# Moving the making of a bias column from the head of the program into the middle of a LayerNorm

## Chip, cores, metric

One core of one Trainium2 chip. The metric is the device time of one execution in microseconds, all four layers from inputs in HBM to the output in HBM. A profile's span runs from the program's first instruction to its last; the device time is about 1.8 us more.

In lines of the profile, PE is TensorE's matmuls and PEld its weight loads, DVE is VectorE, ACT ScalarE, POOL GpSimd and SP SyncE; L588 is line 588 of the kernel, often that of a helper. LN is LayerNorm, FFN the feed-forward block B.

## The reference

Two kinds of residual block alternate, A B A B, on x of 2048 x 448 in bf16.

```python
x = x + _A_ref(_layernorm(x), A_w_r, A_w_i)        # irfft2(rfft2(LN(x)) * W)
x = x + _B_ref(_layernorm(x), B_w1, B_b1, B_w2, B_b2)   # FFN with squared ReLU
x = x + _A_ref(_layernorm(x), A_w_r, A_w_i)
x = x + _B_ref(_layernorm(x), B_w1, B_b1, B_w2, B_b2)

def _B_ref(x, w1, b1, w2, b2):
    h = einsum("bsd,df->bsf", x, w1) + b1
    r = where(h > 0, h, 0)
    return einsum("bsf,fd->bsd", r * r, w2) + b2
```

"Layer 1" below is the first A and the first B, "layer 2" the second pair.

## The kernel before

The program is not written in the order in which it runs. Every operation is entered with what it reads and writes; a scheduler in the kernel then sorts the operations into one fixed list for each engine, from priorities (`PR`), from letters that say which engine may do an operation (`EN`), and from costs that it assumes. On the chip each engine works through its list in order and waits on semaphores. The scheduler also fills gaps of TensorE with matmuls on a tile of ones ("fillers", line 1157), to keep its clock up.

The parts that matter here are the transfers at the head, the small unit that turns b1 (14 rows of 128) into a column for each of the 14 blocks of F, and the loop of the first LN:

```python
        dma("act", FA_sb[:], dc["FA"])                           # 64 KB
        dma("act", b1r, B_b1.rearrange("(f p) -> f p", p=P))     # 3.5 KB
        dma("act", J_sb[:], dc["J"])                             # 32 KB, exchange matrix
        for e, a, b in (("sp", 0, 2), ("sp", 2, 4), ("sp", 4, 8), ("sp", 8, 12), ("sp", 12, 16)):
            dma(e, x_sb[:, a:b, :], x_dram[:, a:b, :], slow=1.5)
        # ...
        def b1_columns():
            q = _Tile(1)
            mm(q[lambda b: ps[:, b, 0:FB]], b1r, J_sb[0:FB, P - FB:P][:, ::-1], True, True)
            cp(b1T[:, 0:FB], q[lambda b: ps[:, b, 0:FB]])
        # ...
        for q in range(8):                     # LN of layer 1, two tiles at a time
            rank("A1", 0, q)
            ln_stats([2 * q, 2 * q + 1], True) # VectorE; tiles 1, 3, 11 on ScalarE
            ln_rstd([2 * q, 2 * q + 1])
            first_A(2 * q)                     # Fs = FA * rstd, 5 matmuls, evacuation to XA
            first_A(2 * q + 1)
        rank("aux", 0, 0)
        b1_columns()
        spectral(True)
```

`FA_sb`, `TD_sb` and `TI_sb` hold constant matrices of the transforms: Fs is FA scaled for one tile of x, XA takes what the matmuls with Fs give, a matmul with TD opens the spectral stage, and one with TI comes after it. `b1T` is first used by the FFN of layer 1. In the lists that the scheduler made, the b1 matmul stands behind TensorE's sixth filler, and the copy is the fourth instruction of VectorE, ahead of all statistics.

Of the kernel before, what the change touches and what calls it, by code (L numbers as in the profile page):

```python
# [10 lines left out]
P = 128  # L11
# [8 lines left out]
FB = 14  # L20
# [95 lines left out]
EN = {'lny': ['addbdbadb', 'aadbdadbb'], 'A1x': ['brxprrdr'], 'A1f': ['xrpxprbp'], 'A1e': ['abbbbaab'], 'A2s': ['dbbabbabadbbbddb'], 'A2e': ['abaabababdaadbaa'], 'TDe': ['adbbababb', 'abadaaaad'], 'Be': ['bbbabbbaa', 'abaaabaaa'], 'Bie': ['baaaadaab', 'aaaaabbda'], 'TIe': ['adbbbbaaa', 'aabdabbbb'], 'fle': ['badababdb', 'bddaabaab']}  # L116
# [77 lines left out]
def _res(a):  # L194
    return a.ap() if isinstance(a, _PsAP) else a
# [303 lines left out]
def _free(ap):  # L499
    n = 1  # L500
    for step, cnt in list(ap.ap)[1:]:
        n *= cnt
    return n


def bass_interleave_layers__spectral_gfnet__dense_activation_squared_relu__prompt_kernel(nc, A_x, A_w_r, A_w_i, B_x, B_w1, B_b1, B_w2, B_b2, out):
# [6 lines left out]
    with ExitStack() as es:  # L513
        onchip = set()

        def sb(name, shape, dt=BF16):
            t = es.enter_context(nc.sbuf_tensor(name, shape, dt))
            onchip.add(t.name)
            return t
# [10 lines left out]
        xb = arena[:, 2 * FB * 512:2 * FB * 512 + NT * D].rearrange("p (t d) -> p t d", t=NT)  # L530
# [15 lines left out]
        J_sb = sb("J_sb", [P, P])  # L546
        Fs = sb("Fs", [P, NFS, 2 * P])
        m2 = sb("m2", [P, NT, 4])
        ones = sb("ones", [P, P])
        W1_sb = sb("W1_sb", [P, 4, FF])  # L550
        b1r = Z[0:FB, 7, 3, 0:P]
# [10 lines left out]
        ps = es.enter_context(nc.psum_tensor("ps", [P, NB, 512], FP32))  # L562
# [24 lines left out]
        def mm(o, lhsT, rhs, start, stop, skip=False, half=False, unit=None):  # L587
            op = sch.add("pe", lambda e: e.matmul(_res(o), lhsT, rhs, start=start, stop=stop, skip_group_check=skip),  # L588
                         [lhsT, rhs], [o], cost=max(_free(rhs) / 2.4 + 2.5, 48.0) * (0.5 if half else 1.0), lat=195.0,
                         unit=unit)  # L590
            if half:
                op.mode = "half"
            return op
# [21 lines left out]
        def rank(k, L=None, n=None):  # L615
            if L is not None:
                at[:] = L, n
            sch.bias = PR[k][at[0]][at[1]]

        def evac(o, i, key):  # L620
            engs = ENG[EN[key][at[0]][at[1]]]
            rank(key)
            n = _free(o)
            far = isinstance(i, _PsAP)
            c = {"act": (n + (61.0 if far else 112.0)) / 1.2, "dve": n / 0.96 + 69.0 if far else n / 3.84 + 60.0,
                 "pool": n + 69.0}
            h = []
            op = sch.add("act", lambda e: e.activation(o, _res(i), ACT.Copy) if h[0].eng == "act" else  # L628
                         e.tensor_copy(o, _res(i)), [i], [o], cost=c["act"])  # L629
            h.append(op)  # L630
            op.alt = {e: c[e] for e in engs}

        def scaled(o, i, s, key):
            engs = ENG[EN[key][at[0]][at[1]]]
            rank(key)
            n = _free(o)
            c = {"act": (n + 112.0) / 1.2 + 93.0, "dve": n / 3.84 + 130.0, "pool": 0.83 * n + 245.0}
            h = []
            op = sch.add("act", lambda e: e.activation(o, i, ACT.Copy, scale=s) if h[0].eng == "act" else
                         e.tensor_scalar(o, i, s, 1.0, op0=ALU.mult, op1=ALU.mult), [i, s], [o], cost=c["act"])  # L640
            h.append(op)
            op.alt = {e: c[e] for e in engs}
# [5 lines left out]
        def cp(o, i, eng="dve"):  # L648
            rate = 0.96 if isinstance(i, _PsAP) or eng == "pool" else 1.92
            sch.add(eng, lambda e: e.tensor_copy(o, _res(i)), [i], [o], cost=_free(o) / rate + 69.0)  # L650
# [27 lines left out]
        for i in range(2):  # L678
            o = Wa[1 - i::2, 17 * WC + 1:33 * WC + 1]
# [51 lines left out]
        def b1_columns():  # L731

            q = _Tile(1)
            mm(q[lambda b: ps[:, b, 0:FB]], b1r, J_sb[0:FB, P - FB:P][:, ::-1], True, True)
            cp(b1T[:, 0:FB], q[lambda b: ps[:, b, 0:FB]])
# [48 lines left out]
        def first_A(t):  # L784

            f = Fs[:, t % NFS, :]
            scaled(f, FA_sb[:], rstd[:, t, 0:1], "A1f")
            rank("A1m")
            q = _Tile(1)
            F2 = f[:, None, 0:P].to_broadcast([P, 2, P])  # L790

            def o(k):
                return q[lambda b: ps[:, b, 2 * P * k:2 * P * (k + 1)]]

            for k in range(2):
                mm(o(k), x_sb[:, t, D0[k]:D0[k] + P], F2, k == 0, False, skip=True)
                mm(o(k), xr[:, t, D0[k]:D0[k] + P], f, False, False, skip=True)
            mm(q[lambda b: ps[:, b, :].rearrange("p (k g c) -> p k g c", k=2, g=2)[:, :, 0, :]],
               m2[:, t, 0:1].to_broadcast([P, P]), F2, False, True, skip=True)
            A_out(t, q, "A1e")  # L800
# [150 lines left out]
        def normed(o, x, i, free):  # L951
            m, r, a = mv[:, i, 0:1], rstd[:, i, 0:1], sd[:, i, 3:4]
            if not free:
                ts(o, x, m, r, ALU.subtract, ALU.mult)
                return
            engs = ENG[EN["lny"][at[0]][at[1]]]
            h = []
# [180 lines left out]
        for q in range(8):  # L1138
# [4 lines left out]
# [4 lines that stand above are left out]
        ffn(False)  # L1147
# [93 lines left out]
```

## Time and profile before

| | before |
|---|---|
| time, median of 3 (range) | 269.78 us (269.03 to 270.4) |
| span of the profile | 269.0 us |
| VectorE's first statistics start | 7.79 us |
| LN of layer 1, from there to the first matmul on TD_sb | 16.28 us |
| spectral stage of layer 1, to the first matmul on TI_sb (46.07) | 22.00 us |
| rest, to the end | 222.9 us |

The last four rows are the frame: they add up to the span. The page's first part (busy us, share of the span, instructions) has TensorE at 96%, with fillers counted as work:

```profile
PE 257.3 (96%) x2383; PEld 163.9 (61%) x2383; DVE 202.7 (75%) x704; ACT 184.6 (69%) x392; POOL 11.0 (4%) x24
```

### The profile page before, as it was taken

Reading aid. Unit: us, or ns where it says so; the run is one execution under the profiler, and the core shown is the slowest. Engines: PE = TensorE matmul, PEld = TensorE weight load, DVE = VectorE, ACT = ScalarE, POOL = GpSimd, SP = SyncE. Lnnn points to the kernel's source line nnn. Section 1 sums busy time; section 2 is a strip of 40 time slices with the busy share of each in tenths; the row PEclk is TensorE's granted clock in tenths of the full one; section 3 lists DMA queues with packets and bytes.
Section 4 is the critical chain, followed back from the end, with each engine's and each line's share of the span. In section 5 each row is a group of like instructions: output and inputs, shape, how many; then the busy total and the mean of one; then the engine's idle time right before and its main releaser. Section 6 shows DMA issues by size and latency. Waiting matters only on the chain.

```text
span 269.0 us, 6410 instructions
## 1 busy us (share of the span) xinstructions
PE 257.3 (96%) x2383; PEld 163.9 (61%) x2383; DVE 202.7 (75%) x704; ACT 184.6 (69%) x392; POOL 11.0 (4%) x24
## 2 busy tenths in 40 slices
PE   4899999999999999999999999998999999999996
PEld 1477997785755554444567986776754544554454
DVE  0784998999999998556599899799899855213622
ACT  4397997995889368783387998877989785005700
POOL 4361000000000000000000000000000000000000
PEclk9999999999999999999999999999999999999999
DMA  6999990003733730004000000002056200010011
GB/s 195 407 347 369 356 340 8 0 2 92 137 130 98 131 125 0 2 0 141 0 2 0 2 1 2 4 0 41 20 109 132 47 0 20 34 53 19 0 37 51
DMA packets 24474, 23.25 MB, mean 86 GB/s; under 512 B 16284, under 2 KB 20988, under 8 KB 24316
## 3 DMA queue, kind: packets, MB, share of 16 engines
q1 hardware_dynamic: 23968, 21.82, 27.3%
q0 software_dynamic: 160, 0.92, 0.8%
q8 instruction: 19, 0.31, 0.5%
q10 hardware_dynamic: 316, 0.10, 0.2%
q14 instruction: 11, 0.09, 0.1%
HBM read 15.49 MB, written 2.76 MB: 68 GB/s over the span
## 4 chain that ended last, share of the span: by engine, by line
PE 79%; ACT 10%; DVE 5%; DMA 4%; issue 1%; ACTq 0%
PE ps L588 77%; ACT XA L628 3%; ACT arena L628 3%; DMA J_sb<-c_J 2%; DMA yT<-xin 2%; PE ps L1157 2%; ACT tmp L628 1%; DVE arena L646 1%; ACT mv L611 1%; DVE x_raw L936 1%; DVE st L966 1%; ACT VT L628 1%; DVE tmp L629 0%; ACTq L583 0%; DVE x_raw L938 0%
## 5 line engine op out<-in xcount | busy, mean ns | idle before, releaser
L611 ACT ACTIVATE arena<-ps,b1T 128x512 bf16<-128x512 f32 (+1 forms) x140 | 74.0, 614 | 31.2 <-PE ps L588 30.9
L588 PE MATMUL ps<-yT,W_sb 64*128 64x512 bf16 (+1 forms) x980 | 87.1, 333 | 1.0 <-DMA yT<-xin 0.7
L588 PE MATMUL ps<-W_sb,arena 128*128 128x448 bf16 (+1 forms) x476 | 86.8, 342 | 0.0
L588 PEld LDWEIGHTS ps<-yT,W_sb 64*128 64x128 bf16 x980 | 50.3, 94 | 37.3 <-ACT arena L611 5.1
L588 PEld LDWEIGHTS ps<-W_sb,arena 128*128 128x128 bf16 x476 | 46.1, 98 | 37.8 <-DVE arena L646 0.8
L646 DVE TENSOR_TENSOR arena<-arena 128x512 bf16<-128x512 bf16 (+1 forms) x140 | 47.9, 367 | 19.1 <-ACT arena L611 18.7
L1055 DVE TENSOR_TENSOR x_raw<-ps,arena 128x448 bf16<-128x448 f32 (+1 forms) x23 | 13.3, 579 | 20.8 <-PE ps L588 20.8
L628 ACT ACTIVATE arena<-ps 128x896 bf16<-128x896 f32 (+1 forms) x32 | 25.6, 905 | 2.5 <-PE ps L588 2.5
L1157 PE MATMUL ps<-ones 128*128 128x512 bf16 x54 | 17.1, 440 | 1.1 <-DVE ones L659 1.1
L628 ACT ACTIVATE VT<-ps 128x512 bf16<-128x512 f32 x28 | 16.2, 680 | 2.7 <-PE ps L588 2.7
L628 ACT ACTIVATE XA<-ps 128x512 bf16<-128x512 f32 x30 | 16.3, 595 | 2.6 <-PE ps L588 2.4
L646 DVE TENSOR_TENSOR arena<-tmp 128x896 bf16<-128x896 bf16 (+1 forms) x32 | 17.1, 591 | 0.3
L738 ACT ACTIVATE tmp<-x_raw 128x448 bf16<-128x448 bf16 x14 | 8.0, 574 | 13.4 <-DVE x_raw L1051 13.3
L588 PE MATMUL ps<-H_sb,arena 128*128 128x128 bf16 x256 | 16.5, 219 | 0.5 <-DVE arena L646 0.5
L738 ACT ACTIVATE VT<-x_raw 128x448 bf16<-128x448 bf16 x24 | 13.8, 582 | 4.3 <-DVE x_raw L938 4.3
L588 PEld LDWEIGHTS ps<-H_sb,arena 128*128 128x128 bf16 x256 | 14.8, 98 | 2.5 <-DVE arena L646 2.5
L646 DVE TENSOR_TENSOR tmp<-VT 128x224 bf16<-128x224 bf16 (+1 forms) x56 | 16.2, 318 | 0.2
L938 DVE SCALAR_TENSOR_TENSOR x_raw<-ps,x_raw 128x448 bf16<-128x448 f32 x24 | 14.3, 616 | 0.8 <-PE ps L588 0.8
L588 PE MATMUL ps<-arena,G_sb 128*128 128x224 bf16 x128 | 14.3, 259 | 0.1
L628 ACT ACTIVATE tmp<-ps 128x896 bf16<-128x896 f32 (+1 forms) x16 | 12.7, 853 | 1.9 <-PE ps L588 1.9
L611 ACT ACTIVATE mv<-mv,epst 128x2 f32<-128x2 f32 (+1 forms) x31 | 9.1, 300 | 5.6 <-DVE mv L752 4.4
L588 PEld LDWEIGHTS ps<-arena,G_sb 128*128 128x128 bf16 x128 | 11.9, 98 | 0.7 <-ACT arena L628 0.6
(77 smaller groups left out, 266.2 us busy)
## 6 DMA issues: line engine op xcount, KB each, us to landing
W_sb<-in_B_w_dram SPq DMA_DIRECT2D x2, 896.0 KB, 6.5
out_dram<-x_raw SPq DMA_DIRECT2D x15, 112.0 KB, 1.7
W_sb<-in_B_w_dram SPq DMA_DIRECT2D x1, 1568.0 KB, 12.7
x_raw<-in_A_x_dram SPq DMA_DIRECT2D x3, 448.0 KB, 6.2
H_sb<-c_H SPq DMA_DIRECT2D x1, 1088.0 KB, 9.3
yT<-xin SPq DMA_DIRECT2D x4, 225.0 KB, 5.3
Wrev<-xin SPq DMA_DIRECT2D x2, 450.0 KB, 10.4
xin<-Wrev SPq DMA_DIRECT2D x4, 225.0 KB, 3.8
```

Source lines behind the costliest of these rows:

```text
L588: op = sch.add("pe", lambda e: e.matmul(_res(o), lhsT, rhs, start=start, stop=stop, skip_group_check=skip), [lhsT, rhs], [o], cost=max(_fr ...
L611: sch.add("act", lambda e: e.activation(o, _res(i), func, **kw), rd, [o], cost=c)
L628: op = sch.add("act", lambda e: e.activation(o, _res(i), ACT.Copy) if h[0].eng == "act" else e.tensor_copy(o, _res(i)), [i], [o], cost=c[" ...
L646: sch.add(eng, lambda e: e.tensor_tensor(o, _res(a), b, op), [a, b], [o], cost=_free(o) / rate + 69.0)
L738: sch.add("act", lambda e: e.activation(o, x, ACT.Square, accum_out=sd[:, t, 1:2]), [x], [o, sd[:, t, 1:2]], cost=560.0)
L936: sch.add("dve", lambda e, xx=xx, xi=xi, r=r: e.tensor_tensor(xx, _res(r), xi, ALU.add), [r, xi], [xx], cost=536.0)
L938: small(lambda e, xx=xx, xi=xi, r=r, i=i: e.scalar_tensor_tensor(out=xx, in0=_res(r), scalar=1.0, in1=xi, op0=ALU.mult, op1=ALU.add, accum ...
L966: small(lambda e, i=i: e.bn_stats(st[:, i, 0:6], x_sb[:, i, 0:D]), [x_sb[:, i, 0:D]], [st[:, i, 0:6]], 536.0)
L1055: sch.add("dve", lambda e: e.tensor_tensor(o, _res(i), xb[:, t, d0:d1], ALU.add), [i, xb[:, t, d0:d1]], [o], cost=(d1 - d0) / 0.96 + 69.0)
L1157: return lambda e: e.matmul(ps[:, b, :], ones[:], ones[:, None, :].to_broadcast([P, 4, P]), start=True, stop=True)
```

## The change

Intent: TensorE and VectorE should not meet the transfers of J and b1 before these have landed. The b1 matmul is told that it reads a column of m2 that the LN of tiles 10 and 11 writes. It does not; the false read only keeps the scheduler from placing it earlier. The priorities of the first LN and of layer 1's spectral stage, and the engine letters for them, are new as well.

```diff
-        def mm(o, lhsT, rhs, start, stop, skip=False, half=False, unit=None):
+        def mm(o, lhsT, rhs, start, stop, skip=False, half=False, unit=None, also=()):
             op = sch.add("pe", lambda e: e.matmul(...),
-                         [lhsT, rhs], [o], cost=...
+                         [lhsT, rhs, *also], [o], cost=...
@@ b1_columns
-            mm(..., b1r, J_sb[0:FB, P - FB:P][:, ::-1], True, True)
+            mm(..., b1r, J_sb[0:FB, P - FB:P][:, ::-1], True, True, also=[m2[:, 10, 0:1]])
@@ tables, cut: of PR the first list of TD, B, W, Bi, TDe, Be, Ws, Bie and all of A1, aux, A1x, A1f, A1m, A1e; of EN, shown as ..., the first word of TDe, Be and Bie
-EN = {..., 'A1x': ['brxprrdr'], 'A1f': ['xrpxprbp'], 'A1e': ['abbbbaab'], ...}
+EN = {..., 'A1x': ['bbxqpxda'], 'A1f': ['drxxprdq'], 'A1e': ['baaaaaad'], ...}
```

More of the change, by code (lines that the diff above doesn't have):

```diff
@@ L111, in make_constants @@
                 J=np.eye(P)[::-1])
-PR = {'TD': [[1510607, 1492741, 1491034, 1343318, 1393964, -3615858, 1398823, 973064, 1485741], [2520683, -882130, 2513278, 1403817, -946609, -1006157, -1079382, -1083072, 1408461]], 'B': [[1485140, 1514860, 1501477, 1399358, 1504936, -3591466, 1503956, -3590078, 961566], [2513805, -1004943, 1405526, 2514030, 1385417, -1091018, 967616, -1128168, -974908]], 'W': [[1849139, 1836802, 1884322, 1860165, 1860418, 981529, 1855478, 1880484, 986484], [258958, 196705, -32086, -31831, 199273, -68617, -58145, -231565, -289839]], 'Bi': [[992350, -3627728, -3593143, -3606899, -3606153, -3597099, -3606581, -3605094, -3596021], [-1103789, 969189, -981009, 1254540, 970491, 1105225, 1552262, 1255862, 1105109]], 'ln': [[991126, 1016681, 13698, -12192, 3592, -9275, 58717, 59319, 60173], [-215928, -161644, -233516, -1278285, -1243220, -1249248, -1270637, -1075997, -1090994]], 'TI': [[4661211, 3603451, 3461865, -3320802, 3581733, -3314912, 3577378, -3303437, -3557233], [1148985, 1261825, -1055731, -1010406, -1074609, -1083367, -1026469, -1043258, -1050048]], 'AI': [[3603697, 4997207, 4997530, 4979074, 3482668, 4986081, 4943161, 4901552, 4992029], [-1080862, 1269571, 943460, -1102619, 1036527, 1203915, -1142225, 1214879, 1183541]], 'xb': [[966, 109389, -75965, -110358, -218149, -39133, -137679, -133462, -146632], [-874934, -227306, -1248899, -1550879, -1543334, -1550645, -1548009, -1575947, -1598280]], 'h': [[4994138, 5003910, 4900585, 4903100, 4901125, 4954442, 5002645], [-1085930, 1201108, 1202903, 1171062, 1082119, 1231856, 1056057]], 'o': [[5025464, 5043598, 4946662, 4825629, 4947511, 4769147, 4931712, 4939797, 4905816, 4965852, 4907640, 4758088, 4928290, 3664542, 4936102, 3571000], [1035960, 1041613, 1046935, 1054242, 1080488, 1155787, 1169102, 1155870, 1000585, 1239792, 1159813, 1159789, 1170072, 1159974, 1163403, 1047019]], 'A2': [[-34871, -450185, -573944, -145705, 153605, 80879, -602905, 81580, 79768, -84049, 81902, 81224, 99503, 452346, 464311, 452106]], 'A1': [[1811154, 1811355, 1842735, 1845662, 1842065, 1842576, 1826448, 1840939]], 'aux': [[1505401, -292702, -154625, 1848161]], 'A1x': [[1811802, 1797921, 1830263, 1787522, 1758506, 1787869, 1798665, 1812907]], 'A1f': [[1815437, 1814986, 1840060, 1843242, 1984370, 1791775, 1844072, 74669]], 'A1m': [[1502233, 1479272, 1517675, 1507165, 1503516, 1518961, 1518966, 1489731]], 'A1e': [[928729, 1815500, 1902353, 928717, 1675923, 1716716, 1675936, 1943634]], 'A2f': [[-34049, -127990, -606838, -439476, -138011, 89305, -571804, 80322, 86631, 80269, 450792, 462862, 54580, 466206, 59337, 450170]], 'A2s': [[480058, 130187, 326278, 591247, -431528, 73495, -83424, -22736, -590315, -851545, -746374, -585928, -115865, -441429, 129400, 466571]], 'A2m': [[4922555, 4746350, 4716000, 4727107, 4938752, 4935914, 4721112, 4719912, 3545281, -1102588, 3449906, 3544553, -1101765, 4721131, 3545586, -1101726]], 'A2e': [[43630, 40194, -682618, -204383, 162475, -55941, 457346, -202207, 210383, 251692, -640306, -43305, -207937, 110571, 278833, 493288]], 'TDe': [[954306, 1843647, 965927, 1000070, 978035, 876912, 1001412, 997131, 1721659], [234287, 1417255, 495995, 497071, -692296, -708408, 116793, 481473, -31496]], 'Be': [[1746203, 1001954, 1683907, 960405, 1780546, 967818, 1669193, 1684490, 963029], [-673471, -562228, -700927, 509333, -668554, 482845, -571588, -638456, -610624]], 'Ws': [[1889039, 1798939, 1854874, 1886651, 814650, 911035, 1938936, 1878593, 1822359], [212971, -52164, -46639, -245211, -58995, -232137, -245502, -184844, -32998]], 'Bie': [[971134, 947163, 1784532, 1001939, 1002073, 987816, 1001937, 1001943, 1001461], [1425225, 487576, -647465, -980124, -655085, -74395, -74265, -181695, -980116]], 'TIe': [[913909, 919877, 722393, -268012, 716509, -288603, 853646, 1008636, 792915], [-149289, -168051, -87569, -1092127, -1364282, -1052619, -148265, -1019412, -75009]], 'AIf': [[-308433, 3579, -182406, 12653, 80551, 7729, -143107, -148725, -142263], [-1045428, -423729, -1430802, -276728, -1103758, -1170272, -918535, -1355679, -1095738]], 'AIs': [[1037824, 921138, 43475, 988, 25617, -29947, -110980, 57417, 53976], [-160854, -145123, -793906, -883581, -1371555, -217899, -1046764, -1245627, -1325531]], 'lnq': [[254432, -546412, 123603, 7472, -193124, -186442, 9410, 836140, -149412], [-287651, -1394001, -1546005, -1125253, -1199492, -1202077, -101648, -1538229, -1522243]], 'lny': [[168910, 899305, 37852, 73400, -12667, 102790, 55869, -23759, 84279], [-244523, -464919, -208553, -1628453, -1450315, -1200119, -1077933, -1545496, -1133605]], 'fl': [[4991518, -3553909, 5045833, 5074410, 3443910, -3419830, 4794596, -3248326, 4963895], [-1100203, -1109390, -1282316, -1178605, -1592271, -1453810, 732254, -1093079, -1088719]], 'fle': [[-189687, 766990, -622264, 878315, -707948, 922239, -284319, -762173, -301700], [-1435726, -776655, -779325, -884711, -359745, -150713, -909732, -337434, -263372]], 'hA': [[-173623, -61538, 82981, 166072, -461795, 94451, 17384], [-59738, -1239374, -1219139, -169082, -1225583, -1223164, -59731]], 'hD': [[24938, -128082, -607193, -606364, -517680, 4299, -81566], [-949150, -1571960, -1533320, -1506174, -1592396, -1567483, -1293058]], 'oD': [[6213, -23599, -603373, -443574, 151235, 130944, 83824, 118459, -119914, 133726, 132035, -4922, 78773, 479772, 77491, 442182], [-1549288, -1077336, -1522386, -1421216, -1499943, -906811, -859800, -1465910, -1534119, -1026687, -1633193, -1551677, -1535519, -1571610, -1461819, -1620002]]}
@@ L116 @@
-EN = {'lny': ['addbdbadb', 'aadbdadbb'], 'A1x': ['brxprrdr'], 'A1f': ['xrpxprbp'], 'A1e': ['abbbbaab'], 'A2s': ['dbbabbabadbbbddb'], 'A2e': ['abaabababdaadbaa'], 'TDe': ['adbbababb', 'abadaaaad'], 'Be': ['bbbabbbaa', 'abaaabaaa'], 'Bie': ['baaaadaab', 'aaaaabbda'], 'TIe': ['adbbbbaaa', 'aabdabbbb'], 'fle': ['badababdb', 'bddaabaab']}
+PR = {'TD': [[1611015, 1560745, 1571669, 1391435, 1398832, -3621416, 1374866, -3479716, 1402951], [2520683, -882130, 2513278, 1403817, -946609, -1006157, -1079382, -1083072, 1408461]], 'B': [[1578993, 1416687, 1553212, 1417621, 1401279, -3584572, -3471848, 1550869, -3659354], [2513805, -1004943, 1405526, 2514030, 1385417, -1091018, 967616, -1128168, -974908]], 'W': [[1833706, 1883605, 1713507, 1845799, 1846051, 1858785, 1847117, 1976414, 992154], [258958, 196705, -32086, -31831, 199273, -68617, -58145, -231565, -289839]], 'Bi': [[-3600236, -3636088, 1397759, -3650383, -3634765, -3649053, -3658753, -3646144, -3576979], [-1103789, 969189, -981009, 1254540, 970491, 1105225, 1552262, 1255862, 1105109]], 'ln': [[991126, 1016681, 13698, -12192, 3592, -9275, 58717, 59319, 60173], [-215928, -161644, -233516, -1278285, -1243220, -1249248, -1270637, -1075997, -1090994]], 'TI': [[4661211, 3603451, 3461865, -3320802, 3581733, -3314912, 3577378, -3303437, -3557233], [1148985, 1261825, -1055731, -1010406, -1074609, -1083367, -1026469, -1043258, -1050048]], 'AI': [[3603697, 4997207, 4997530, 4979074, 3482668, 4986081, 4943161, 4901552, 4992029], [-1080862, 1269571, 943460, -1102619, 1036527, 1203915, -1142225, 1214879, 1183541]], 'xb': [[966, 109389, -75965, -110358, -218149, -39133, -137679, -133462, -146632], [-874934, -227306, -1248899, -1550879, -1543334, -1550645, -1548009, -1575947, -1598280]], 'h': [[4994138, 5003910, 4900585, 4903100, 4901125, 4954442, 5002645], [-1085930, 1201108, 1202903, 1171062, 1082119, 1231856, 1056057]], 'o': [[5025464, 5043598, 4946662, 4825629, 4947511, 4769147, 4931712, 4939797, 4905816, 4965852, 4907640, 4758088, 4928290, 3664542, 4936102, 3571000], [1035960, 1041613, 1046935, 1054242, 1080488, 1155787, 1169102, 1155870, 1000585, 1239792, 1159813, 1159789, 1170072, 1159974, 1163403, 1047019]], 'A2': [[-34871, -450185, -573944, -145705, 153605, 80879, -602905, 81580, 79768, -84049, 81902, 81224, 99503, 452346, 464311, 452106]], 'A1': [[2017417, 2016753, 2017368, 2018568, 2015776, 2016320, 2011733, 2013388]], 'aux': [[1784077, 2030436, 1458000, -222125]], 'A1x': [[-78438, 1764055, 2017145, 1740521, 1945455, 2017149, 1733606, 2013750]], 'A1f': [[2026475, 2022846, 1700588, 1673326, 1885756, 2013682, 1843661, 1757672]], 'A1m': [[1624402, 1624407, 1618344, 1618039, 1618053, 1537576, 1602322, 1670734]], 'A1e': [[2018288, 1743124, 2013324, 2018938, 1792872, 2007452, 926476, 1834891]], 'A2f': [[-34049, -127990, -606838, -439476, -138011, 89305, -571804, 80322, 86631, 80269, 450792, 462862, 54580, 466206, 59337, 450170]], 'A2s': [[480058, 130187, 326278, 591247, -431528, 73495, -83424, -22736, -590315, -851545, -746374, -585928, -115865, -441429, 129400, 466571]], 'A2m': [[4922555, 4746350, 4716000, 4727107, 4938752, 4935914, 4721112, 4719912, 3545281, -1102588, 3449906, 3544553, -1101765, 4721131, 3545586, -1101726]], 'A2e': [[43630, 40194, -682618, -204383, 162475, -55941, 457346, -202207, 210383, 251692, -640306, -43305, -207937, 110571, 278833, 493288]], 'TDe': [[2015312, 1881608, 1834874, 1912279, 933173, 1914329, 1811666, 1807467, 2012655], [234287, 1417255, 495995, 497071, -692296, -708408, 116793, 481473, -31496]], 'Be': [[1810378, 2015630, 1839426, 1797362, 938200, 1031040, 933515, 1076416, 1026320], [-673471, -562228, -700927, 509333, -668554, 482845, -571588, -638456, -610624]], 'Ws': [[1843817, 1846443, 1875937, 2003156, 1836055, 1861290, 2004506, 1857296, 1821747], [212971, -52164, -46639, -245211, -58995, -232137, -245502, -184844, -32998]], 'Bie': [[1820631, 1817640, 1818170, 1921951, 1076577, 1873067, 1921957, 1027958, 1022790], [1425225, 487576, -647465, -980124, -655085, -74395, -74265, -181695, -980116]], 'TIe': [[913909, 919877, 722393, -268012, 716509, -288603, 853646, 1008636, 792915], [-149289, -168051, -87569, -1092127, -1364282, -1052619, -148265, -1019412, -75009]], 'AIf': [[-308433, 3579, -182406, 12653, 80551, 7729, -143107, -148725, -142263], [-1045428, -423729, -1430802, -276728, -1103758, -1170272, -918535, -1355679, -1095738]], 'AIs': [[1037824, 921138, 43475, 988, 25617, -29947, -110980, 57417, 53976], [-160854, -145123, -793906, -883581, -1371555, -217899, -1046764, -1245627, -1325531]], 'lnq': [[254432, -546412, 123603, 7472, -193124, -186442, 9410, 836140, -149412], [-287651, -1394001, -1546005, -1125253, -1199492, -1202077, -101648, -1538229, -1522243]], 'lny': [[168910, 899305, 37852, 73400, -12667, 102790, 55869, -23759, 84279], [-244523, -464919, -208553, -1628453, -1450315, -1200119, -1077933, -1545496, -1133605]], 'fl': [[4991518, -3553909, 5045833, 5074410, 3443910, -3419830, 4794596, -3248326, 4963895], [-1100203, -1109390, -1282316, -1178605, -1592271, -1453810, 732254, -1093079, -1088719]], 'fle': [[-189687, 766990, -622264, 878315, -707948, 922239, -284319, -762173, -301700], [-1435726, -776655, -779325, -884711, -359745, -150713, -909732, -337434, -263372]], 'hA': [[-173623, -61538, 82981, 166072, -461795, 94451, 17384], [-59738, -1239374, -1219139, -169082, -1225583, -1223164, -59731]], 'hD': [[24938, -128082, -607193, -606364, -517680, 4299, -81566], [-949150, -1571960, -1533320, -1506174, -1592396, -1567483, -1293058]], 'oD': [[6213, -23599, -603373, -443574, 151235, 130944, 83824, 118459, -119914, 133726, 132035, -4922, 78773, 479772, 77491, 442182], [-1549288, -1077336, -1522386, -1421216, -1499943, -906811, -859800, -1465910, -1534119, -1026687, -1633193, -1551677, -1535519, -1571610, -1461819, -1620002]]}
@@ L117 @@
+EN = {'lny': ['addbdbadb', 'aadbdadbb'], 'A1x': ['bbxqpxda'], 'A1f': ['drxxprdq'], 'A1e': ['baaaaaad'], 'A2s': ['dbbabbabadbbbddb'], 'A2e': ['abaabababdaadbaa'], 'TDe': ['ddabaabaa', 'abadaaaad'], 'Be': ['aabbaabbb', 'abaaabaaa'], 'Bie': ['bbabadaaa', 'aaaaabbda'], 'TIe': ['adbbbbaaa', 'aabdabbbb'], 'fle': ['badababdb', 'bddaabaab']}
 ENG = {"a": ("act",), "d": ("dve",), "p": ("pool",), "b": ("act", "dve"), "q": ("act", "pool"), "r": ("dve", "pool"),
@@ L585, in dma @@
                         lat=slow * 2.0 * n / sch.DMA_RATE)
-        def mm(o, lhsT, rhs, start, stop, skip=False, half=False, unit=None):
+        def mm(o, lhsT, rhs, start, stop, skip=False, half=False, unit=None, also=()):
             op = sch.add("pe", lambda e: e.matmul(_res(o), lhsT, rhs, start=start, stop=stop, skip_group_check=skip),
-                         [lhsT, rhs], [o], cost=max(_free(rhs) / 2.4 + 2.5, 48.0) * (0.5 if half else 1.0), lat=195.0,
+                         [lhsT, rhs, *also], [o], cost=max(_free(rhs) / 2.4 + 2.5, 48.0) * (0.5 if half else 1.0), lat=195.0,
                          unit=unit)
@@ L733, in b1_columns @@
             q = _Tile(1)
-            mm(q[lambda b: ps[:, b, 0:FB]], b1r, J_sb[0:FB, P - FB:P][:, ::-1], True, True)
+            mm(q[lambda b: ps[:, b, 0:FB]], b1r, J_sb[0:FB, P - FB:P][:, ::-1], True, True, also=[m2[:, 10, 0:1]])
             cp(b1T[:, 0:FB], q[lambda b: ps[:, b, 0:FB]])
```

## The prediction

> **What bounds the kernel now.** I read the page first, then the chain of waits in order of time, then the waits of the first 8 us, then the timeline of the start, then busy time by stage.
>
> The page's chain says that TensorE carries most of the span, and one small transfer stands in it as well:
>
> ```profile
> PE 79%; ACT 10%; DVE 5%; DMA 4%; issue 1%; ACTq 0%
> PE ps L588 77%; ACT XA L628 3%; ACT arena L628 3%; DMA J_sb<-c_J 2%; DMA yT<-xin 2%; PE ps L1157 2%; ACT tmp L628 1%; DVE arena L646 1%; ACT mv L611 1%; DVE x_raw L936 1%; DVE st L966 1%; ACT VT L628 1%; DVE tmp L629 0%; ACTq L583 0%; DVE x_raw L938 0%
> ```
>
> J_sb is the exchange matrix of 32 KB. The only early user of it is the matmul that turns b1 into columns. The chain in order of time (start, length, what) begins with it:
>
> ```profile
> 1.86 5.50 DMA J_sb<-c_J
> ...
> 7.49 0.17 PE ps L588
> 7.66 3.10 PE ps L1157 x7
> 10.76 2.92 PE ps L588 x15
> ```
>
> The 7 pieces of L1157 are matmuls on ones that only keep the clock up. So nothing useful ran on TensorE before 10.6 us. The waits of the first 8 us (total, times, longest) and the timeline show who stood still:
>
> ```profile
> DVE b1T L650 <- PE ps L588: 6.7, 1, 6.7
> PE ps L588 <- DMA J_sb<-c_J: 3.6, 1, 3.6
> ```
>
> ```profile
> 3.64 0.57 ACT L746 ACTIVATE tmp<-x_raw 128x448 bf16<-128x448 bf16 x1
> ...
> 7.46 0.10 PEld L588 LDWEIGHTS ps<-J_sb,arena 14*128 14x128 bf16 x1 [4.53 <-issue]
> 7.49 0.17 PE L588 MATMUL ps<-J_sb,arena 14*128 14x14 bf16 x1 [3.65 <-DMA J_sb<-c_J]
> ...
> 7.70 0.17 DVE L650 COPY b1T<-ps 128x14 f32<-128x14 f32 x1 [6.65 <-PE ps L588]
> 7.79 0.62 DVE L758 BATCH_NORM_STATS2 st<-x_raw 128x6 f32<-128x448 bf16 x1
> ```
>
> The reader is to see two things. ScalarE reads tile 1 of x at 3.64, so the first x transfer (tiles 0 and 1) has landed by then. VectorE begins its first statistics only at 7.79, because the b1T copy stands ahead of it in its program. ScalarE then waits in turn: it has 4.05 us of idle time before the first square root (9.62), which needs VectorE's variance.
>
> Busy time by stage (stretch, length, then PE, PEld, DVE, ACT, POOL, clock, DMA share, GB/s): the stall, the LN in two parts, and layer 1's spectral stage:
>
> ```profile
> 3.64:7.79 4.15, 0.50 (x3) 0.23 (x3) 0.09 (x2) 1.90 (x7) 2.58 (x3) 1.00 0.89 286
> 7.79:14.74 6.95, 6.95 (x31) 3.63 (x30) 5.55 (x25) 3.39 (x9) 2.50 (x5) 1.00 0.99 394
> 14.74:24.07 9.33, 8.67 (x68) 6.08 (x67) 6.76 (x34) 9.01 (x24) 4.77 (x10) 1.00 0.98 343
> 24.07:46.07 22.00, 21.70 (x263) 19.93 (x264) 20.09 (x38) 19.32 (x30) 0.00 (x0) 1.00 0.75 269
> ```
>
> From 14.74 to 24.07 ScalarE is busy 9.01 of 9.33 us: it ends the LN. PE's 6.95 of 6.95 in the row before is mostly filler. From 24.07 on TensorE is the bound (21.70 of 22.00).
>
> **What the Trainium skill says.** "TensorE: Matmul & The Clock Gate", the engine queue depths under "Architectural detail": ScalarE and VectorE are strict FIFO, TensorE can only pull weight loads ahead. The trace agrees: VectorE did nothing for 6.65 us with x on chip for 4.15 of them. "DMA: Bandwidth & Descriptors", section "Issuing engines are not separate DMA queues": transfers issued by different engines interleave on the same 16 DMA engines. The trace agrees: J_sb, issued from ScalarE, took 5.50 us for 32 KB, while FA_sb with 64 KB, issued first, took 2.5. Same page, "Rules for kernel authors": issue early and wait late; the change does the second half of that. "TensorE: Matmul & The Clock Gate", Part 1: an idle TensorE runs at half rate until some 3.4 us of activity. The trace agrees in kind: the 256-column matmuls start 0.21 us apart until 13.0 us and 0.11 apart after it, 5.5 us after TensorE resumed.
>
> **The change, part by part.**
> 1. One false read is added to the b1 matmul: column 10 of m2, which is written in the LN of tiles 10 and 11. The matmul (0.17 us) and the copy (0.17 us) move from the head of TensorE's and VectorE's programs to a place after five of eight LN pairs, near 12 to 16 us, when J_sb (landed 7.36) and b1 have long been there. Nothing is removed: 0.2 us or less returns there, on engines that are not the bound of that stretch. The first user of b1T runs at 55.8 us.
> 2. Head of the program: VectorE's statistics can begin at 3.64 instead of 7.79. That is 7.79 - 3.64 = 4.15 us. TensorE doesn't idle for 3.65 us, so its clock should be up by about 7 us.
> 3. Does the LN keep its length? It ran 16.3 us (7.79 to 24.07). ScalarE's work from 3.64 to the LN's end is 1.90 + 3.39 + 9.01 = 14.3 us, VectorE's 5.55 + 6.76 = 12.3. In the old order 1.90 us of ScalarE's work was done during the stall; in the new order it must fit beside the first statistics. It should: from 7.79 to the first evacuation (11.91) ScalarE worked 0.20 + 0.56 + 0.19 + 0.30, about 1.3 of 4.1 us, so 2.8 us are free for the 1.90. If x comes in time the LN ends at 24.07 - 4.15 = 19.9. The floor by ScalarE's work is 3.64 + 14.3 = 17.9, so up to 2 us more could be had from better order.
> 4. The priorities and engine letters of layer 1's LN and spectral stage are new. The evacuations of the last pair go to VectorE by name ("d"), one more per pair may: about 2 x 0.6 = 1.2 us off ScalarE's end. VectorE has 9.33 - 6.76 = 2.6 us of room. I book 0.5 us for it, an estimate, because the gains of such a reorder were likely mostly aimed at what part 2 opens.
> 5. Spectral stage: its matmuls are the same. 22.00 us hold 7 fillers (1.08 + about 0.5 us); I book 0.1 of net change. From 46 us on nothing is edited; TI, AI, FFN and layer 2 keep their priorities and should move as one block.
> 6. Cost of x arriving: tiles 4 to 7 landed at 7.17, 8 to 11 at 8.3, 12 to 15 at 9.4. VectorE's work on tiles 0 to 3 took from 7.79 to 11.6, 3.8 us, so it would be ready for tile 4 at 3.64 + 3.8 = 7.45, after 7.17. I book -0.2 us for small waits.
> Sum: 4.15 + 0.5 + 0.1 - 0.2 = 4.55 us. 269.78 - 4.55 = 265.2 us.
>
> **The rivals.**
> Transfers take over. The DMA engines are at 0.98 to 1.00 from 8 us on, and they don't get faster. If the spectral stage comes 4.5 us early, it may meet its own loads. Against it: the second range of W landed at 24.9 us and is first used at about 33.0; the last piece of H landed at 28.0 and is used at about 38.7. Shifted by 4.5, the uses come at 28.5 and 34.2, with 3.6 and 6.2 us of slack. The first range of W landed at 16.0, its first use moves from 27.2 to 22.7. TD_sb landed at 11.2. If I am wrong on one, 1 to 3 us go back: 266.5 to 268.5.
> The LN is bound by ScalarE and by x, not by the start. Then removing the stall only lets VectorE run ahead and wait later, and the gain is perhaps 2 to 3 us, 267 to 268. For it: ScalarE's 97% in the second part. Against it: ScalarE was idle 4.05 us waiting for VectorE's first result, so its own start was held by the same stall.
> The new order gets more than the shift. A warm clock from the first real matmul halves the first three tiles' 1.06 us each, and ScalarE's load moves to VectorE and GpSimd. The LN could then end at 18.5 to 19 and the gain be 5.5 us: 264.3, just over 2%.
> Nothing at all, because TensorE is 96% busy: its early busy time is filler, so I give this little.
>
> **Range and chances.** Two per cent of 269.78 is 5.4 us, that is 264.4. The sum is 4.55, and its uncertain terms (order -1 to +1.5, loads down to -2) give 263.6 to 267.0 for 8 in 10. Faster by over 2%: 0.24. Within 2%: 0.75. Slower by over 2% would need the later block to be scheduled differently and worse: 0.01.
>
> **What would show it right or wrong.** Right: VectorE's first statistics start at 3.6 to 3.8; no wait of b1T over 0.3 us; J_sb is gone from the chain; the first matmul from TD_sb is at 19 to 20.5 instead of 24.07; from there to the end the distance is 245 us as now, within 1. If the LN starts early but TD still starts after 21.5, the ScalarE rival holds. If VectorE's products with W or the H matmuls wait for transfers between 20 and 36 us, the transfer rival does. If the distance from the TD stage to the end grows by over 1 us, the block did not move as one, and my step 5 is wrong.

## The result

| | before | changed |
|---|---|---|
| time, median | 270.08 us (269.03 to 270.4, 4 runs) | 265.84 us (265.78 to 265.88, 4 runs) |
| ratio, 95% interval | | 0.985 (0.9821 to 0.9879) |
| span of the profile | 269.0 | 264.1 |
| first statistics | 7.79 | 3.54 |
| LN of layer 1 | 16.28 | 15.63 |
| spectral stage | 22.00 | 22.00 |
| rest | 222.9 | 222.9 |

Ratios here and below are the mean time of one kernel's runs over that of the other's of the same rounds, so not quite the ratio of the medians quoted. Executions over 1.5% slower than the fastest of the same kernel are left out of the means. The kernel is about 1.5% faster, inside 2%.

The waits of the first 8 us in the changed kernel (total, times, longest): no line of b1T or J_sb is left, and VectorE's wait is now for x itself.

```profile
DVE st L758 <- DMA x_raw<-in_A_x_dram: 2.5, 1, 2.5
...
ACT mv L611 <- DVE mv L752: 0.6, 1, 0.6
```

The chain of waits in order of time (start, length, what) no longer starts with a transfer. It starts with fillers, and the first real matmul comes at 6.63 instead of 10.65:

```profile
1.10 5.43 PE ps L1157 x14
6.53 0.10 issue
6.63 2.48 PE ps L588 x20
...
10.38 0.49 POOL Fs L640
...
11.00 3.24 PE ps L588 x27
...
17.82 1.15 ACT XA L628 x2
18.98 0.20 issue
19.17 15.98 PE ps L588 x189
```

The timeline of VectorE shows the copy where it went, without idle time before it:

```profile
3.54 0.63 DVE L758 BATCH_NORM_STATS2 st<-x_raw 128x6 f32<-128x448 bf16 x1 [2.50 <-DMA x_raw<-in_A_x_dram]
...
15.92 0.14 DVE L650 COPY b1T<-ps 128x14 f32<-128x14 f32 x1
```

Busy time by stretch (stretch, length, then PE, PEld, DVE, ACT, POOL, clock, DMA share, GB/s), the rest of the program before and after:

```profile
46.07:269.00 222.93, 216.89 (x2016) 133.32 (x2016) 169.98 (x604) 149.55 (x323) 0.00 (x0) 1.00 0.18 43
```

```profile
19.17:41.17 22.00, 21.52 (x262) 19.83 (x263) 20.04 (x38) 19.23 (x30) 0.00 (x0) 1.00 0.98 347
41.17:264.10 222.93, 216.89 (x2016) 133.27 (x2016) 170.00 (x604) 149.58 (x323) 0.00 (x0) 1.00 0.18 43
```

All of the 4.9 us between these two profiles lies ahead of the spectral stage: 4.25 us in the start of the statistics, 0.65 us in the length of the LN. From 19.17 on the program moved as one block. The medians differ by less, 4.24 us (before's is of four runs here, one more than the prediction knew). The profile of before is not quite typical: its run took 270.76 us, more than any of the four, and run 11 shows what made its LN longer.

### The profile page after: what moved, and what is told of

Its sections match the earlier page's. It is cut to its first block, busy times and chain, and to the rows that moved or that the text cites. A ratio compares the mean times of both kernels' runs of the same rounds, so it can differ in the third digit from the quotient of the medians.

```text
span 264.1 us, 6399 instructions
## 1 busy us (share of the span) xinstructions
PE 255.7 (97%) x2383; PEld 163.3 (62%) x2383; DVE 204.3 (77%) x708; ACT 183.8 (70%) x391; POOL 9.5 (4%) x21
## 3 DMA queue, kind: packets, MB, share of 16 engines
HBM read 15.49 MB, written 2.76 MB: 69 GB/s over the span
## 4 chain that ended last, share of the span: by engine, by line
PE 82%; DVE 7%; ACT 7%; DMA 2%; issue 1%; POOL 0%; POOLq 0%; DVEq 0%
PE ps L588 79%; ACT arena L628 3%; PE ps L1157 2%; DVE arena L646 2%; DMA yT<-xin 2%; ACT XA L628 2%; ACT tmp L628 1%; DVE tmp L646 1%; DVE x_raw L936 1%; DVE st L966 1%; ACT VT L628 1%; DVE tmp L629 0%; DVE x_raw L938 0%; DVE VT L646 0%; ACT mv L611 0%
## 5 line engine op out<-in xcount | busy, mean ns | idle before, releaser
L628 ACT ACTIVATE arena<-ps 128x896 bf16<-128x896 f32 (+1 forms) x32 | 26.3, 911 | 2.6 <-PE ps L588 2.6
L1157 PE MATMUL ps<-ones 128*128 128x512 bf16 x54 | 16.4, 428 | 1.1 <-DVE ones L659 1.1
L628 ACT ACTIVATE XA<-ps 128x512 bf16<-128x512 f32 x28 | 15.2, 593 | 2.4 <-PE ps L588 2.4
L758 DVE BATCH_NORM_STATS2 st<-x_raw 128x6 f32<-128x448 bf16 (+1 forms) x19 | 10.9, 589 | 2.5 <-DMA x_raw<-in_A_x_dram 2.5
```

Of the source, the lines that this page charges most:

```text
L628: op = sch.add("act", lambda e: e.activation(o, _res(i), ACT.Copy) if h[0].eng == "act" else e.tensor_copy(o, _res(i)), [i], [o], cost=c[" ...
L758: small(lambda e, si=si, xi=xi: e.bn_stats(si, xi), [xi], [si], _free(xi) / 0.96 + 69.0)
L1157: return lambda e: e.matmul(ps[:, b, :], ones[:], ones[:, None, :].to_broadcast([P, 4, P]), start=True, stop=True)
```

## Experiments

Theory: J's landing holds the head of the program, and the gain is the time that is no longer lost there. Rivals: the new priorities and letters make the gain; ScalarE or the loads bound the LN, so that the head has slack; a removed wait is only displaced. Two questions came up on the way: which of the two engines' stops counts, and why kernels with the same head differ by up to 1 us. Each kernel was timed in five rounds unless said, beside runs of before on the same chip. All results were correct but one.

### 1. The false read alone

The changed kernel with the old `PR` and `EN`. The lists differ from those of before in the place of the b1 matmul (with its fillers) and of the copy, and in nothing else.

```diff
-PR, EN = <new tables>
+PR, EN = <tables of before>
```

> The false read alone, with the old priorities and letters: the order of both programs differs only in where the b1 matmul and its copy stand. Head-stall theory: VectorE's first statistics start at 3.5 to 3.7 us in place of 7.8, the first TD matmul comes near 19.8, and the time is 4.1 to 4.3 us under before, 265.7 to 266.4. Rival, the new order of layer 1 makes the gain: at most 1 to 2 us are gained here, 268 to 269. Rival, ScalarE bounds the LN: VectorE starts early but TD comes after 21.5, 267 to 268.

265.04 us (264.93 to 265.64) beside 269.92; ratio 0.983 (0.9814 to 0.9847). Statistics at 3.59, TD at 19.01. The gain is whole, even 0.7 us more than I expected of it. TensorE's timeline:

```profile
19.01 1.22 PE L588 MATMUL ps<-TD_sb,XA 128*128 128x224 bf16 x11 [0.30 <-ACT XA L628]
```

The rival of the new order and the rival of ScalarE's bound fall with this run.

### 2. The new tables alone

```diff
-            mm(..., True, True, also=[m2[:, 10, 0:1]])
+            mm(..., True, True)
```

> The new priorities and letters without the false read, so that the b1 matmul and its copy stand at the head again. Head-stall theory: the statistics start at about 7.8 as before, and only the 0.65 us by which the LN got shorter show: 269.0 to 269.7. Rival, the new order makes the gain: 266 to 267.

270.44 us (269.62 to 271.27), ratio 1.0016 (0.9995 to 1.0036): nothing. J landed at 8.04 in this profile, the statistics start at 8.47, TD comes at 23.96. The 0.65 us that I thought the new order had won in the LN do not show.

### 3. J first in ScalarE's queue

```diff
-        dma("act", FA_sb[:], dc["FA"])
-        dma("act", b1r, ...)
         dma("act", J_sb[:], dc["J"])
+        dma("act", b1r, ...)
+        dma("act", FA_sb[:], dc["FA"])
```

> The kernel before with the three transfers that ScalarE issues in the order J, b1, FA instead of FA, b1, J; the order on TensorE and VectorE is that of before. If only the landing of J counts: J lands at about 3.2 (as FA does now), statistics start at 3.7 to 4.2, time 265.8 to 266.6, nearly all of the gain without moving an instruction. If b1's own transfer (second in the queue in both) is late too, or J is slow wherever it stands: the statistics start at 5 to 7.5 and the time is 268 to 270.

268.72 us (267.47 to 269.04), ratio 0.9948 (0.9928 to 0.9968). I had the first half right and the time wrong. J landed at 3.11, the b1 matmul ran at 3.77, the statistics started at 4.09. But FA, now third, landed at 7.96, and the scaling of FA had to wait for it. The waits of the first 12 us and the chain of waits show most of the loss again, under a new name:

```profile
DVE Fs L640 <- DMA FA_sb<-c_FA: 1.2, 1, 1.2
```

```profile
1.86 6.10 DMA FA_sb<-c_FA
7.96 0.03 issue
7.99 0.30 DVE Fs L640
8.29 0.14 issue
8.42 3.21 PE ps L588 x15
```

This is the displaced wait of the rivals, though not of this change: it comes from moving a transfer, not from moving its user. In every profile where its landing is recorded, a transfer of 128 rows in that third place landed 0.17 to 0.35 us behind the x transfer of tiles 4 to 7, which was issued just before it.

### 4. More stall in place of less

The kernel before, same lists, with one wait more at the b1 matmul: TD_sb, which landed at 11.19 in the first profile.

```diff
+        sch.b1[0].deps.append(sch.td)    # the landing of TD_sb; cut: where sch.b1 and sch.td are set
         sch.assign_tickets()
```

> The kernel before, same order of every engine, with one more semaphore wait ahead of the b1 matmul: it waits for TD_sb as well, which landed at 11.19 us in the profile of before. Head-stall theory (each us of stall is a us of time): statistics start at about 11.6, 3.8 us later than before, and the time is 3.6 to 4.0 us over before, 273.6 to 274.2. If the LN had slack or were bound by transfers or by ScalarE's total work: under 2 us more.

273.07 us (271.31 to 275.17), ratio 1.0137 (1.0102 to 1.0172): clearly slower, by about 3 us, a little under what I expected. The profiled run was the fastest one; there TD_sb landed at 9.23, the statistics began at 9.65 and TD came at 25.40. VectorE's timeline:

```profile
9.56 0.17 DVE L650 COPY b1T<-ps 128x14 f32<-128x14 f32 x1 [8.52 <-PE ps L588]
```

Between the place-only kernel and this one the statistics move by 6.06 us (3.59 to 9.65) and TD by 6.39 us (19.01 to 25.40): a microsecond of stall is about a microsecond of time. The wide spread would fit a head that waits for a transfer, though only the profiled run has its landing on record; the changed kernel's runs lie within 0.1 us in its first comparison and within 0.9 us in run 7.

### 5. b1 in the third place

```diff
         dma("act", FA_sb[:], dc["FA"])
-        dma("act", b1r, ...)
         dma("act", J_sb[:], dc["J"])
+        dma("act", b1r, ...)
```

> The kernel before with ScalarE's three transfers in the order FA, J, b1. In the run with J first, FA stood third and landed at 7.97, 0.25 us after the x transfer of tiles 4 to 7. Theory, it is the third place that is late (whatever is issued at 1.86 us lands just behind that 448 KB transfer): b1, with 3.5 KB, is late in J's place, the statistics start at 7 to 8.5 us and the time is that of before, 269.5 to 270.5. Rival, lateness goes with J's or FA's size or rows: b1 lands by 4, statistics start at 4.1, time 265.0 to 266.

266.94 us (266.74 to 269.57), ratio 0.9894 (0.9857 to 0.993). Both were wrong: the b1 matmul waited 1.80 us for b1 and ran at 5.64, not at 4 and not after 7. So b1 was late there, but some 2 us less than the 128 rows of J or FA. Two things differ: b1 has 14 rows, and its transfer was issued at 1.59 us, ahead of the 448 KB of x (issued at 1.65), while J and FA in the third place were issued at 1.86, behind them. Which of the two made the 2 us no run shows.

### 6. No need of J

The kernel before, same lists and transfers. The b1 matmul multiplies by a corner of the tile of ones and waits for b1 alone. The bias is wrong (relative error 0.26).

```diff
+        # cut: b1 matmul's deps lose J's landing and gain the tile of ones; and
+        sch.b1[0].fn = lambda e: e.matmul(ps[:, t.bank, 0:FB], b1r, ones[0:FB, 0:FB], start=True, stop=True)
         sch.assign_tickets()
```

> The kernel before, same order of every engine and same transfers, but the b1 matmul multiplies by a corner of the tile of ones instead of J, so it waits for b1 alone. The bias is wrong on purpose, so the result may be wrong. Theory, J's landing alone holds the head: the matmul runs at about 3.8, statistics start at 4.1, no other wait takes its place (FA is first in the queue here), and the time is 265.0 to 265.9. Rival, a wait is only displaced, as when J went first: 268 to 269.

266.02 us (266.0 to 266.73), ratio 0.9843 (0.982 to 0.9866). Statistics at 4.09, as expected; the time is 0.1 us over the range. So the early place of matmul and copy costs little by itself; J's landing was nearly the whole price. TensorE's timeline:

```profile
3.78 0.19 PE L1163 MATMUL ps<-ones,arena 14*128 14x14 bf16 x1
```

### 7 and 8. The changed kernel and the place-only kernel side by side

No edit; both again.

> The changed kernel itself, beside the next run on the same chip. Theory, the new priorities and letters are worth nothing or cost a little: 265.7 to 265.9, as in its own runs, and slower than the place-only kernel by 0.2 to 0.8.

> The place-only kernel once more: 265.0 to 265.7. Its profile had a transpose transfer of layer 2 of 3.7 us where the changed kernel's had 4.8, and its runs fell in two groups, 264.9 to 265.0 and 265.6. If that transfer makes the difference to the changed kernel, a profile with 4.8 us here goes with a span of 263.8 to 264.0, and one with 3.5 to 3.8 us with 263.0 to 263.2; if the new tables make it, the transfer does not matter and the spans stay at 263.1.

Changed: 265.78 us (265.21 to 266.11), ratio 0.983. Place only: 265.62 us (265.48 to 265.76), ratio 0.9827. They are the same. LN lengths agree too: 15.64 and 15.56 us. So what made 265.04 of run 1? Its profile's rest was 222.1 us, not 222.9, and the difference begins at one point of layer 2, where TensorE waits for the first transposing transfer of the FFN (yT<-xin). In run 1 that transfer took 3.75 us, in this repeat 4.78, and the span went from 263.1 to 264.0. The waits from 170 to 185 us, run 1 first, then its repeat:

```profile
PEld ps L588 <- DMA yT<-xin: 0.4, 1, 0.4
```

```profile
PEld ps L588 <- DMA yT<-xin: 1.1, 1, 1.1
...
PE ps L588 <- DMA yT<-xin: 0.7, 1, 0.7
```

It was also short (3.49 us) in run 4 and 4.7 to 4.8 in all other profiles. The same place-only kernel shows both lengths, so the change doesn't make the difference. Only one run of each was profiled; that the faster group of run 1's runs is this transfer is likely, not shown. What makes it short is open.

### 9. A place that is not late enough

The place-only kernel with the false read on tile 0's column.

```diff
-            ..., also=[m2[:, 10, 0:1]])
+            ..., also=[m2[:, 0, 0:1]])
```

> The place-only kernel with the false read on tile 0's column of m2 instead of tile 10's: the b1 matmul stands after ten of the fillers and the copy ten places into VectorE's program, some 5.3 us, still ahead of J's landing (7.4 to 8.1). Theory (a stall is what is missing between the program's arrival at the copy and J's landing): statistics start at 3.5, a wait of 2.3 to 3.0 us stands before the copy, and the time is 267.3 to 269.0, between place-only and before. Rival, any place but the very head is good enough: 265.0 to 265.8.

269.44 us (268.31 to 269.87), ratio 0.9962 (0.9936 to 0.9988). The wait before the copy is 2.81 us as expected, but nearly all of the gain is gone, more than the theory allowed. VectorE's timeline:

```profile
8.25 0.17 DVE L650 COPY b1T<-ps 128x14 f32<-128x14 f32 x1 [2.81 <-PE ps L588]
```

What I had left out is TensorE. It stood still for 2.5 us behind ten fillers, and afterwards its first 15 real matmuls took 3.37 us in the chain, where 20 took 2.48 us in the changed kernel: its clock had fallen (granted 0.50 from 9.36 to 12.73). How much of the loss is VectorE's wait and how much TensorE's clock this run doesn't say.

### 10. The transfers moved too

The place-only kernel with b1 and J loaded from SyncE's queue behind TD_sb.

```diff
-        dma("act", b1r, ...)
-        dma("act", J_sb[:], dc["J"])
@@
-        dma("sp", TD_sb[:], dc["TD"])
+        dma("sp", TD_sb[:], dc["TD"]); dma("sp", b1r, ...); dma("sp", J_sb[:], dc["J"])
```

> The place-only kernel with the transfers of b1 and J moved as well, from ScalarE's queue at the head to SyncE's behind TD_sb: their user comes at 15.6 us. Gains that could still lie there: ScalarE's table load starts about 1 us earlier, and x meets two transfers less. Theory, both are hidden (ScalarE's first pass waits for x at 3.5, b1 and J are 35.5 KB beside 1.8 MB): 265.0 to 265.7, as place-only, with the statistics at 3.4 to 3.6. Rival, b1 and J slowed the x transfers: tiles 4 to 7 land by 6.5 and the time is 264.3 to 264.9.

265.59 us (265.56 to 266.06), ratio 0.9833: as place-only, as expected. ScalarE's table load starts at 1.12 instead of 2.24, and then it waits for x until 3.46. Nothing is gained there. No run but run 1 beats the changed kernel clearly, and run 1's 0.8 us did not come back in run 8.

### 11. The kernel before once more (three rounds)

> The kernel before itself, as a control and for a second profile of it: ratio 1.000 within 0.004. Theory for its LN of 16.28 us in the first profile: part of it is TensorE's clock, which stayed low until 13.2 us. If so the LN's length here goes with the time at which its 256-column matmuls come to 0.11 us apart: about 15.5 us where that is at once, 16.3 where it takes 2.5 us. Statistics start at J's landing plus 0.43, spectral stage 22.00, rest 222.9 or 222.1.

270.52 us (269.64 to 271.33), ratio 1.002 (0.9989 to 1.005). The control holds. Its profiled run was a fast one, and the LN took 15.15 us, not 16.28. In the first profile the 256-column matmuls with Fs started 0.21 us apart until 13.17 us; here they start 0.11 us apart from the first one on (10.70 us). Clock and LN length go together, as expected. Busy time from 7.80 to 13.20 shows it by the number of matmuls in 11.00:13.20, 13 in the first profile and 21 here (columns as above):

```profile
7.80:11.00 3.20, 3.20 (x9) 1.04 (x8) 2.84 (x17) 0.99 (x4) 0.00 (x0) 1.00 1.04 415
11.00:13.20 2.20, 2.20 (x13) 1.50 (x11) 1.96 (x6) 0.98 (x3) 1.65 (x4) 1.00 0.99 400
```

```profile
7.80:11.00 3.20, 3.20 (x10) 1.06 (x9) 2.89 (x17) 0.94 (x4) 0.00 (x0) 0.55 1.03 415
11.00:13.20 2.20, 2.20 (x21) 1.72 (x20) 1.92 (x6) 1.93 (x5) 1.60 (x4) 1.00 1.01 407
```

The record of the clock in this run has three entries at the head: full from 3.83, half from 7.24, full from 10.65, each 3.41 us apart. The stop of TensorE from 3.8 to 7.5 cost it its clock: such a half entry at the head stands in the profiles of runs 3, 9 and 11 alone, where an entry of full came before or within a stop of 2.5 us or more, and in none of those without such a stop in the first 10 us (changed, 1, 6, 7, 8, 10). When the clock comes back differs from run to run on that grid, which can be part of why this kernel's times spread over 1 to 2 us; that was not tested by itself.

In this profile the chain from J's landing to the end of the LN runs through VectorE's copy and statistics, and not through the fillers as in the first profile:

```profile
7.54 0.18 PE ps L588
7.75 0.17 DVE b1T L650
7.92 0.54 DVE st L758
```

### 12. The wait on TensorE alone

The place-only kernel, same lists; TensorE's seventh filler, where the b1 matmul stood in the kernel before, waits for J. VectorE waits for nothing new.

```diff
+        sch.ops["pe"][6].deps.append(sch.j)    # J's landing; cut: where sch.j is set
         sch.assign_tickets()
```

> The place-only kernel with one wait put back, on TensorE alone: its seventh filler, where the b1 matmul stood in the kernel before, waits for J. VectorE waits for nothing new: its statistics start at 3.5. If TensorE's stop is enough (the fillers behind it run in order, so the first matmul with Fs comes at 10.6 to 11.1, and ScalarE's program stands at its first evacuation until then): the gain is nearly lost, 268.3 to 270.0. Rival, it was VectorE's copy that cost the time and TensorE's stop only delays work with slack, because the statistics run ahead: 265.6 to 267.0.

269.90 us (269.29 to 271.37), ratio 0.9984 (0.9954 to 1.0014): the gain is gone. The statistics start at 3.57, and it doesn't help. The first matmul with Fs comes at 10.79, because eight fillers stand behind the wait, at low clock. ScalarE, in order, stands at its first evacuation. The waits of the first 12 us, and ScalarE's timeline:

```profile
PE ps L1157 <- DMA J_sb<-c_J: 3.6, 1, 3.6
```

```profile
12.10 2.41 ACT L628 ACTIVATE XA<-ps 128x512 bf16<-128x512 f32 x4 [4.81 <-PE ps L588]
```

### All profiles in the frame

First statistics and LN in us; the spectral stage took 22.00 to 22.07 in all of them.

| run | first statistics | LN | rest | span |
|---|---|---|---|---|
| before, first profile | 7.79 | 16.28 | 222.90 | 268.97 |
| before, run 11 | 7.84 | 15.15 | 222.85 | 267.85 |
| changed | 3.54 | 15.63 | 222.92 | 264.09 |
| 1 place only | 3.59 | 15.42 | 222.13 | 263.15 |
| 7 changed again | 3.45 | 15.64 | 222.91 | 263.99 |
| 8 place only again | 3.51 | 15.56 | 222.90 | 263.98 |
| 2 tables only | 8.47 | 15.49 | 222.92 | 268.87 |
| 3 J first | 4.09 | 17.95 | 222.91 | 266.95 |
| 4 late b1 | 9.65 | 15.74 | 222.12 | 269.52 |
| 5 b1 third | 5.95 | 15.16 | 222.77 | 265.93 |
| 6 no J | 4.09 | 15.97 | 222.87 | 264.94 |
| 9 read of tile 0 | 3.64 | 19.57 | 222.87 | 268.09 |
| 10 loads late | 3.46 | 15.48 | 222.82 | 263.77 |
| 12 TensorE waits | 3.57 | 20.10 | 222.89 | 268.62 |

## Why the prediction was right or wrong, point by point

The time, 265.84 us, lies in the range and 0.6 us from the predicted 265.2; the gain was 4.24 us by the medians instead of 4.55. Its signs came as well: no wait of b1T, J_sb gone from the chain, TD at 19.17, and 244.9 us from there to the end; only the start of the statistics, 3.54, is 0.06 us before the stated 3.6.

- Step 1, the b1 unit is free where it went: right. The copy took 0.14 us at 15.92 with no wait, the matmul ran at 13.29.
- Step 2, 4.15 us at the head: right, 4.25 us in the profiles, and shown by runs 1, 2 and 4. But I let it rest on VectorE, with TensorE's share as a matter of clock only. Run 12 shows that TensorE's stop alone, with its fillers behind it, costs as much as the whole. Freeing VectorE alone would not have been enough; runs 6 and 8 have in common that both engines' stops are gone. VectorE's stop alone, with TensorE free, was not tried; in run 11 the chain runs through it, so it is not shown to be harmless.
- Step 3, the LN keeps its length: right within half a microsecond, but the 16.28 us that I measured it against held a slow clock. Beside run 11's 15.15 us the changed LN is longer by 0.48 us, beside the first profile shorter by 0.65.
- Step 4, 0.5 us booked for the new order: this is the term that failed. It measured nothing: run 2 gave a ratio of 1.0016, and run 7 beside run 8 shows no gain of the tables with the false read in. Without it the sum would have been 4.05 us and 265.7. The work did move: VectorE has two of the 16 evacuations to XA, and ScalarE's busy time in the LN is 13.66 us in the changed kernel and 14.11 in run 1. What failed is that a shorter ScalarE ends the LN sooner. In run 1 ScalarE's evacuations end the chain (the line below); in the changed kernel the chain runs through GpSimd's scaling of FA and TensorE instead (10.38 and 11.00 in the chain above), and the LN is as long, 15.63 us beside 15.42 and 15.56.

```profile
16.43 2.49 ACT XA L628 x5
```

- Step 5, the spectral stage and all behind it move as one block: right, 22.00 us and 222.93 us before and after. The stage lost one of its 7 fillers, but the 0.1 us booked for that did not come.
- Step 6, x arriving late, -0.2 us: seen in one profile. In run 8 tiles 4 to 7 landed at 7.86 and the statistics of tile 4 start at 7.88, 0.4 us after the start of the instruction before; in run 1 and the changed kernel that is 0.2 us, without idle time. Over all runs it is not separable.
- The rival of transfers that take over did not hold in the changed kernel; it did hold where a transfer was moved instead of its user (run 3). The rival of ScalarE's bound and the one of more than 2% did not hold.

## What to carry to other kernels

A one-off operation at the head of in-order lists can cost the whole lateness of its slowest input, however short it is, and on every engine that has a part in it; here TensorE's stop alone did. If its result is needed late, place it late, behind the moment at which its inputs have landed in the trace (run 9: a little later is not enough). Moving the user was safer here than hurrying the transfer, because the place in the queue stayed late and something else then stood in it (run 3). When a change brings both a moved dependency and new tables, test them apart: here one of them did everything.

## What the Trainium skill lacked or had wrong

- "TensorE: Matmul & The Clock Gate", Part 1: the free-running window agrees with what was seen (entries 3.41 us apart in run 11), but the page, which warns that clock entries can be unreliable, does not say how the profile shows the clock before its first entry. In the first profile of before the clock column says 1.00 for 7.80 to 11.00, while filler matmuls start 0.43 us apart and 256-column matmuls 0.21 us apart there; the first entry in the record is at 13.17 us. Here the spacing of the matmuls tells the clock, not the column.
- "DMA: Bandwidth & Descriptors", "Issuing engines are not separate DMA queues": the page says that transfers of different engines interleave. It gives no figure for how late a small one gets behind a large one: 32 KB of J (or 64 KB of FA in its place), issued from ScalarE 0.2 us after 448 KB of x from SyncE, landed only 0.17 to 0.35 us behind the 448 KB, 4.8 to 6.2 us after its issue, against 2.2 to 2.7 us for FA when first.
- No page has this: one transposing transfer, of the same shape at the same place of the program, took 3.5 to 3.75 us in two profiles and 4.7 to 4.8 us in the others, and moved the end by 0.8 us. Its cause is open.
